# One core, attention beside a token-mixing MLP: the last K tokens ahead of the w2 load, wo in eight loads, a third oT buffer with the wo jobs spread anew

## The chip, the cores and the metric

The kernel runs on one core of a Trainium2 chip. The metric is device time in microseconds (us); lower is better. Most executions of one kernel agree within 0.3%. A difference of 2% or more counts as "faster" or "slower", less as "same". All runs named here are of the state "fast".

Engines: PE is TensorE's matrix multiplication, PEld its weight load, DVE is VectorE, ACT is ScalarE, POOL is GpSimd, SP the engine that issues nearly all transfers. "SPq" lines in the profile are instructions of SP's sequencer. PSUM is the memory, in banks, that TensorE writes its results to; a bank has to be copied out before it can be written anew. Of the names in the profile, `ps_all` is PSUM, `xs` a block of tokens before its transposition, `xnK` and `xnT` the transposed tokens, `kT` and `qT` keys and queries, `pT` the exponentials of the softmax, `ost` the weighted values as copied out of PSUM, `o_s` a unit's output and `oT` its transpose.

## The reference, cut to what matters

```python
def reference(A_x, A_wq, A_wk, A_wv, A_wo, A_beta, B_x, B_w1, B_b1, B_w2, B_b2):
    x = A_x                       # [1, 2048, 1024]
    xn = _layernorm(x, axis=-1)
    return x + _A_ref(xn, A_wq, A_wk, A_wv, A_wo, A_beta) + _B_ref(xn, B_w1, B_b1, B_w2, B_b2)
# _A_ref: 32 heads of 32, the 2048 tokens in 4 segments of 512. Per segment: causal softmax
#   attention inside the segment, plus a read of a compressive memory M, z that holds
#   elu+1 of the earlier segments' keys against their values; gated; then o @ wo.
# _B_ref: layernorm again, then a mixer over tokens: 2048 -> 3584 -> 2048 with gelu, w1, w2.
```

## The kernel before

The program has three stretches: the first mixer product (w1), the second one (w2, and with it the K projection of tokens 1024 to 2047), and attention in 32 *units* (4 segments of 8 groups of 4 heads). All engines are programmed from one place. What the whole case turns on is the order of each engine's queue: in the traces here an instruction that waits holds up what stands behind it (VectorE did nothing from 224.27 to 231.57 us before one instruction, as shown below, though the next one needed nothing that was missing after about 228.8 us, when experiment 2 runs it).

The normalised tokens for the K projection are made by `k_prepare`, which is called after each of the seven products of a w2 step. `n` counts those calls. A token block is scaled on VectorE, then transposed by a DMA. Then four differences (`kD`, operands of a fast multiplication with seven products instead of eight) are made on VectorE:

```python
    TOKENS_AT = (2, 3, 5, 6, 8, 9, 11, 12)
    def k_prepare(self, i, p):
        n = 7 * i + self.ORDER.index(p)
        if n in self.TOKENS_AT:
            ...
            self.xn_scale(c, F16)                                  # VectorE
            self.fw.dma(self.xnK[...], self.xs[c % 4][:], ..., transpose=True, own=True)
        if n - 2 in self.TOKENS_AT[:4]:
            self.xn_load(12 + self.TOKENS_AT.index(n - 2))
        n -= 7 * (self.K_FIRST - 1)
        if 0 <= n < 4:
            self.differences(self.kB, self.R_kB, self.kD, self.R_kD, (n + 1,))
        ...
```

The load of w2 for the step after next (1.8 MB) is issued at calls 5, 12, and so on, just ahead of `k_prepare`.

In attention, a unit's dense work (a queue of *jobs* of eight 512-column matmuls each: the q, k and v projections and the wo product) is cut into pieces that fill TensorE between the logits and the weighting by the softmax. Side work for VectorE is popped at certain *stops* inside the jobs:

```python
    def attention(self):
        ...
        for s in range(N_SEG - 1):
            at = [N_GRP * s + 10 + n for n in range(8)] if s < 2 else [26, 27, 28, 29, 30, 30, 31, 31]
            for n, u in enumerate(at):
                self.wo_plan.setdefault(u, []).append((4 * s + n // 2, n % 2))
        ...
        self.load_fin(0)
        self.load_fin(1)
        self.fw.dma(self.wo[:], self.A_wo.rearrange("(jc p) j -> p jc j", p=P), writes=[self.R_wo])
        for u in range(N_UNIT):
            ...
            if u in self.XN_AT[::4]:                 # u = 0, 6, 14
                self.xn_load(xn)
                self.xn_load(xn + 1)
            ...
            self.stops = self.STOPS_FEW if total <= 26 and u >= N_GRP else self.STOPS
            self.dense(cuts[0]); self.logits(u, 0); self.dense(cuts[1], end)
            if u: self.weigh(u - 1, 0)
            self.dense(cuts[2], False)
            if u: self.weigh(u - 1, 1)
            ...
```

(`STOPS_FEW` has more stops than `STOPS`, in spite of its name: it is for units with few jobs.)

## Time and profile before

| | before |
|---|---|
| median of its runs | 665.98 us |
| span of the profiled run | 664.9 us |
| PE busy | 643.0 us, 97% |
| PE idle in all | 21.9 us |

Lines of the profile page: the span, the busy time of the engines, and two rows of the 40 equal slices (16.6 us each; a digit is tenths).

```profile
span 664.9 us, 11143 instructions
...
PE 643.0 (97%) x4560; PEld 303.7 (46%) x4611; DVE 440.9 (66%) x829; ACT 281.7 (42%) x305; POOL 156.0 (23%) x181
...
PE   9999999999999999999999997999999999999987
...
PEclk9999999999999999999999997999999999999999
...
```

TensorE is the engine that bounds the kernel (97% busy), so time is to be won only where it is idle or slow. One slice, the 25th (about 399 to 416 us), shows both: PE busy falls to 7 tenths and so does the granted clock. Next, who waited for whom (engine, what and line, `<-` what ended the wait: total us, times, longest us; `issue` means that the profile names nothing that was waited for):

```profile
...
PE ps_all L198 <- DVE kT L1259: 4.1, 1, 4.1
...
PE ps_all L198 <- DVE part L690: 1.9, 1, 1.9
PE ps_all L198 <- DVE ost L1412: 1.9, 3, 1.1
...
```

The three of TensorE's waits that are shown are for VectorE. The first in time has this history. In the timeline of SP's sequencer (start, duration, what):

```profile
...
221.79 0.44 SPq L220 DMA_DIRECT2D w2s<-in_B_w_dram  x1
222.30 6.20 SPq L220 DMA_TRANSPOSE xnK<-xs  x1
...
```

and of VectorE and TensorE:

```profile
...
231.57 1.23 DVE L664 TENSOR_TENSOR kD<-xnK,xnK 128x2048 f16<-128x2048 f16 x1 [7.30 <-issue]
...
232.71 0.68 DVE L690 TENSOR_TENSOR part<-ps_all,part 128x512 f32<-128x512 f32 x1
...
233.46 2.76 PE L198 MATMUL ps_all<-g,sum 128*128 128x512 f16 x12 [1.90 <-DVE part L690]
...
```

The last K token's transpose was issued at 222.30 us, just behind a w2 load of 1.8 MB, held the sequencer for 6.2 us and landed at 231 us. VectorE had come to the first difference at 224.27 and waited 7.30 us. The view puts that wait down to "issue"; that it was for the token is read from the landing time here, and from experiment 2, where the same wait is put down to the DMA. Behind it in VectorE's queue stood an add (`part<-ps_all`) that frees what TensorE needs, so TensorE stood for 1.90 us.

The second history, at the start of attention:

```profile
...
391.00 0.43 SPq L220 DMA_DIRECT2D wo<-in_A_wo_dram  x1
391.48 1.07 SPq L220 DMA_DIRECT2D xs<-in_A_x_dram  x2
...
401.46 0.55 DVE L1131 TENSOR_SCALAR xs<-xs,ln_mv,ln_rs 128x1024 bf16<-128x1024 bf16 x1 [8.16 <-DMA xs<-in_A_x_dram]
401.93 0.68 DVE L1259 CAST kT<-ps_all 128x512 bf16<-128x512 f32 x1
...
402.76 0.58 PE L198 MATMUL ps_all<-xnT,wq 128*128 128x512 bf16 x1 [4.14 <-DVE kT L1259]
...
406.76 1.46 PE L198 MATMUL ps_all<-xnT,wq 128*128 128x512 bf16 x3
...
```

The load of wo, 2 MB, went out at 391.00 us, the two xs loads behind it at 391.48. They landed at 401.4 us, 10 us later, where the median of such loads is 3.4. VectorE waited 8.16 us to scale xs; the copy of kT stood behind that, and TensorE waited 4.14 us for the PSUM bank that this copy frees. After that, three matmuls take 1.46 us in all, where three took 0.82 elsewhere: they start some 0.43 us apart instead of 0.216. The whole stretch of units 0 and 1 (from one first exponential of an even unit to the next), in the view of stretches:

```profile
...
core 0: us, PE busy (x) PEld busy (x) DVE busy (x) ACT busy (x) POOL busy (x), PEclk, DMA share, GB/s
389.84:410.58 20.74, 15.93 (x123) 6.91 (x124) 7.39 (x18) 11.55 (x10) 4.94 (x8) 0.84 0.83 235
...
```

The mean granted clock (the third number from the end) was 0.84 there, and the pair took 20.74 us, where the next pairs take 15.0. The third of the waits, for the copy of ost, falls for the most part (1.12 us of 1.9) in units 9 and 10.

### The profile page before, as it was taken

Reading aid. Unit: us, or ns where it says so; the run is one execution under the profiler, and the core shown is the slowest. Engines: PE = TensorE matmul, PEld = TensorE weight load, DVE = VectorE, ACT = ScalarE, POOL = GpSimd, SP = SyncE. Lnnn points to the kernel's source line nnn. Section 1 sums busy time; section 2 is a strip of 40 time slices with the busy share of each in tenths; the row PEclk is TensorE's granted clock in tenths of the full one; section 3 lists DMA queues with packets and bytes.
Section 4 is the critical chain, followed back from the end, with each engine's and each line's share of the span. In section 5 each row is a group of like instructions: output and inputs, shape, how many; then the busy total and the mean of one; then the engine's idle time right before and its main releaser. Section 6 shows DMA issues by size and latency. Waiting matters only on the chain.

```text
span 664.9 us, 11143 instructions
## 1 busy us (share of the span) xinstructions
PE 643.0 (97%) x4560; PEld 303.7 (46%) x4611; DVE 440.9 (66%) x829; ACT 281.7 (42%) x305; POOL 156.0 (23%) x181
## 2 busy tenths in 40 slices
PE   9999999999999999999999997999999999999987
PEld 3444444444444444444444443444445445455443
DVE  6975766656654583563745315766988988787885
ACT  7542322322200000110110164778767778788850
POOL 2500000000021122020220211434333444444440
PEclk9999999999999999999999997999999999999999
DMA  9704242332599825727536966967654675445324
GB/s 303 205 1 127 66 125 65 92 99 64 153 251 268 214 87 151 222 65 220 146 107 175 253 178 171 157 146 155 117 128 108 152 165 143 112 112 125 94 69 129
DMA packets 190011, 95.00 MB, mean 143 GB/s; under 512 B 108552, under 2 KB 176136, under 8 KB 189960
## 3 DMA queue, kind: packets, MB, share of 16 engines
q1 hardware_dynamic: 189816, 94.25, 55.7%
q8 instruction: 36, 0.59, 0.4%
q14 instruction: 15, 0.12, 0.1%
q10 hardware_dynamic: 144, 0.03, 0.0%
HBM read 69.23 MB, written 11.53 MB: 121 GB/s over the span
## 4 chain that ended last, share of the span: by engine, by line
PE 55%; DVE 5%; issue 3%; DMA 2%; ACT 1%; SPq 0%; DVEq 0%
PE ps_all L198 55%; DMA xs<-in_A_x_dram 1%; DVE prod L1458 1%; DVE ost L1412 1%; ACT pT L1361 1%; DVE fin L1604 1%; SPq L220 0%; DMA oT<-o_s 0%; DVE fin L1304 0%; DMA xnK<-xs 0%; DVE o_s L1464 0%; DVE srec L1454 0%; DVE mtmp L1225 0%; DVE kT L1259 0%; DVE srec L1455 0%
## 5 line engine op out<-in xcount | busy, mean ns | idle before, releaser
L1361 ACT ACTIVATE pT<-ps_all 128x2048 bf16<-128x2048 f32 x80 | 150.1, 1876 | 52.4 <-PE ps_all L198 52.2
L1365 POOL TENSOR_SCALAR_AFFINE_SELECT pT<-pT 128x512 bf16<-128x512 bf16 x128 | 107.4, 856 | 168.9 <-ACT pT L1361 168.7
L690 DVE TENSOR_TENSOR part<-ps_all,part 128x512 f32<-128x512 f32 x84 | 57.7, 690 | 105.4 <-PE ps_all L198 85.0
L1076 POOL TENSOR_TENSOR part<-part,stg 128x512 f32<-128x512 f32 x24 | 33.0, 1402 | 287.1 <-DVE part L690 287.1
L747 ACT ACTIVATE g<-part,b1c 128x512 f16<-128x512 f32 x36 | 26.0, 722 | 98.8 <-DVE part L690 98.8
L198 PE MATMUL ps_all<-xnT,wq 128*128 128x512 bf16 x241 | 62.1, 386 | 5.4 <-DVE kT L1259 4.1
L198 PE MATMUL ps_all<-wo,oT 128*128 128x512 bf16 (+2 forms) x256 | 63.0, 366 | 1.8 <-DMA oT<-o_s 0.8
L198 PE MATMUL ps_all<-wv,xnT 128*128 128x512 bf16 x242 | 62.9, 380 | 0.6 <-issue 0.2
L695 ACT ACTIVATE part<-ps_all 128x512 f32<-128x512 f32 x24 | 14.0, 596 | 103.3 <-PE ps_all L198 69.2
L1412 DVE CAST ost<-ps_all 128x396 bf16<-128x396 f32 (+2 forms) x96 | 43.6, 472 | 19.6 <-PE ps_all L198 18.7
L198 PEld LDWEIGHTS ps_all<-vA,pT 128*128 128x128 bf16 x1280 | 45.8, 96 | 23.1 <-DVE ost L1412 5.8
L198 PE MATMUL ps_all<-g,sum 128*128 128x512 f16 x224 | 51.0, 379 | 1.9 <-DVE part L690 1.9
L198 PE MATMUL ps_all<-g,w2s 128*128 128x512 f16 x224 | 51.0, 379 | 0.0
L198 PE MATMUL ps_all<-vA,pT 128*128 128x33 bf16 x1280 | 48.7, 178 | 2.3 <-DVE ost L1412 1.9
L198 PE MATMUL ps_all<-gT,sum 128*128 128x512 f16 x224 | 50.3, 379 | 0.0
L198 PE MATMUL ps_all<-h,sum 128*128 128x512 f16 x192 | 45.2, 379 | 0.0
L198 PE MATMUL ps_all<-h,w1s 128*128 128x512 f16 x192 | 44.9, 379 | 0.0
L198 PE MATMUL ps_all<-hT,sum 128*128 128x512 f16 x192 | 43.6, 379 | 0.0
L198 PEld LDWEIGHTS ps_all<-xnT,wq 128*128 128x128 bf16 x256 | 23.2, 98 | 32.1 <-issue 9.4
L1458 DVE TENSOR_TENSOR prod<-ost,srec 128x1024 bf16<-128x1024 bf16 x24 | 36.8, 1533 | 0.0
L198 PE MATMUL ps_all<-qT,kT 32*128 32x384 bf16 (+3 forms) x512 | 31.9, 303 | 4.0 <-ACT pT L1361 1.9
L198 PEld LDWEIGHTS ps_all<-g,sum 128*128 128x128 f16 x224 | 21.9, 98 | 28.6 <-DVE part L690 2.6
(118 smaller groups left out, 852.6 us busy)
## 6 DMA issues: line engine op xcount, KB each, us to landing
w2s<-in_B_w_dram SPq DMA_DIRECT2D x8, 1792.0 KB, 9.1
w1s<-in_B_w_dram SPq DMA_DIRECT2D x12, 1024.0 KB, 5.6
wq<-in_A_wq_dram SPq DMA_DIRECT2D x32, 256.0 KB, 3.4
xs<-in_A_x_dram SPq DMA_DIRECT2D x24, 256.0 KB, 3.4
stg<-in_A_x_dram SPq DMA_DIRECT2D x16, 256.0 KB, 2.9
out_dram<-stg SPq DMA_DIRECT2D x16, 256.0 KB, 3.3
wk<-in_A_wk_dram SPq DMA_DIRECT2D x16, 256.0 KB, 3.7
fin<-out_dram SPq DMA_DIRECT2D x16, 256.0 KB, 3.4
```

Source lines behind the costliest of these rows:

```text
L198: ins = self.nc.tensor.matmul(*args, **kwargs)
L690: self.fw.op("dve", lambda e: e.tensor_tensor(self.tmp[dst][:], self.bank(b), self.tmp[src][:], op=ALU.add), reads=[self.R_bank[b], self.R ...
L695: self.fw.op("act", lambda e: e.activation(self.tmp[dst][:], self.bank(b), ACT.Copy), reads=[self.R_bank[b]], writes=[self.R_tmp[dst]])
L747: self.fw.op("act", lambda e: e.activation(self.gB[f % 2][half][:, f // 2, :], src, ACT.Gelu_apprx_tanh, bias=self.b1c[:, f:f + 1], scale= ...
L1076: fw.op("pool", lambda e: e.tensor_tensor(self.tmp[t][:], self.tmp[t][:], self.stg[k][:, 512 * half:512 * half + 512], op=ALU.add), reads= ...
L1361: fw.op("act", lambda e: e.activation(dst, src, ACT.Exp, scale=SCALE), reads=self.R_bank[0:4], writes=[R[v % 2][kb] for v, kb, _ in blocks ...
L1365: fw.op("pool", lambda e: e.affine_select(d, d, pattern=[[0, 4], [1, P]], compare_op=ALU.is_ge, fill=0.0, base=0, channel_multiplier=-1), ...
L1412: fw.op("dve", lambda e: e.tensor_copy(dst, src), reads=[self.R_bank[b]], writes=[self.R_ost[o][part]])
L1458: fw.op("dve", lambda e: e.tensor_tensor(self.prod[:], ost[:, :, 0:D_HEAD], rec.unsqueeze(2).to_broadcast([P, 32, D_HEAD]), op=ALU.mult), ...
L1604: fw.op("dve", lambda e: e.tensor_tensor(dst, self.ps[:, b, c0:c1], dst.bitcast(F16), op=ALU.add), reads=[self.R_bank[b], R], writes=[R])
```

## The change

The intent: take away these two stalls, and give the last four units, which have less dense work than the others, some of the wo jobs of the units before. For that the output of two segments has to be kept a little longer, hence a third buffer of `oT`. The diff, cut to its core:

```diff
-    TOKENS_AT = (2, 3, 5, 6, 8, 9, 11, 12)
+    TOKENS_AT = (2, 3, 4, 6, 8, 9, 10, 11)
@@ k_prepare
-        if 0 <= n < 4:
-            self.differences(self.kB, self.R_kB, self.kD, self.R_kD, (n + 1,))
+        if 1 <= n < 5:
+            self.differences(self.kB, self.R_kB, self.kD, self.R_kD, (n,))
@@ every use of oT
-   self.oT[s % 2] ... self.R_oT[s % 2]
+   self.oT[s % 3] ... self.R_oT[s % 3]
@@
+    WO_AT = (range(10, 18), (18, 20, 21, 22, 24, 25, 26, 28), (28, 29, 29, 30, 30, 30, 31, 31))
@@ attention
-            at = [N_GRP * s + 10 + n for n in range(8)] if s < 2 else [26, 27, 28, 29, 30, 30, 31, 31]
+            at = self.WO_AT[s]
...
-        self.load_fin(0)
-        self.load_fin(1)
-        self.fw.dma(self.wo[:], self.A_wo.rearrange("(jc p) j -> p jc j", p=P), writes=[self.R_wo])
         for u in range(N_UNIT):
+            if u == N_GRP:
+                ... take "oT2" where stg was; self.oT.append(t); self.R_oT.append(R)
+                self.load_fin(0)
+                self.load_fin(1)
+            if 1 <= u <= N_GRP:
+                self.fw.dma(self.wo[:, u - 1, :], self.A_wo[(u - 1) * P:u * P, :], writes=[self.R_wo[u - 1]])
...
-            if total <= 26:
+            if u < 10 or u >= 14 and total <= 26:
...
-            self.stops = self.STOPS_FEW if total <= 26 and u >= N_GRP else self.STOPS
+            self.stops = self.STOPS_FEW if total <= 26 and u >= 14 else self.STOPS
```

The title leaves the last two changed lines out. No unit below 14 changes its cuts (units 10 to 13 have 32 matmuls, the others at most 24), but units 8 and 9 go from the many stops to the few.

More of the change, by code (lines that the diff above doesn't have):

```diff
@@ L1181, in before_attention @@
         elif p == 2:
-            self.wo, (self.R_wo,) = take("wo", [P, N_GRP, D_MODEL], BF16)
+            self.wo, self.R_wo = take("wo", [P, N_GRP, D_MODEL], BF16, N_GRP)
         elif p == 3:
@@ L1189, in before_attention @@
             self.xnT[1], self.R_xnT[1] = take("xnT1", [P, N_DCH, SEG_L], BF16, 4)
-            w = _Walk(self.mem, self.B_AT, self.B_AT + self.STG_AT)
+            w = _Walk(self.mem, self.B_AT, self.B_AT + self.S2_AT)
             self.MZ32, self.R_MZ32 = w.take("MZ32", [P, N_GRP, GW], F32, N_GRP)
@@ L1298, in mm @@
         def mm(b, j):
-            self.fw.mm(self.bank(b), self.oT[s % 2][:, j, (c % 4) * P:(c % 4 + 1) * P],
+            self.fw.mm(self.bank(b), self.oT[s % 3][:, j, (c % 4) * P:(c % 4 + 1) * P],
                        self.wo[:, j, half * 512:(half + 1) * 512], start=(j == 0), stop=(j == N_GRP - 1))
@@ L1308, in end @@
                 self.load_fin(c + 2)
-        return [0, None, lambda: [self.R_wo] + self.R_oT[s % 2], mm, end, True]
+        return [0, None, lambda: self.R_wo + self.R_oT[s % 3], mm, end, True]
     def load_fin(self, c):
@@ L1472, in o_transpose_dma @@
         s, g, o = u // N_GRP, u % N_GRP, u % 2
-        self.fw.dma(self.oT[s % 2][:, g, :].rearrange("p (q t) -> p q t", q=4),
+        self.fw.dma(self.oT[s % 3][:, g, :].rearrange("p (q t) -> p q t", q=4),
                     self.o_s[o][:].rearrange("p q j -> p (q j)"),
-                    reads=[self.R_os[o]], writes=[self.R_oT[s % 2][g]], transpose=True)
+                    reads=[self.R_os[o]], writes=[self.R_oT[s % 3][g]], transpose=True)
     def o_transpose(self, u, b):
@@ L1483, in o_transpose @@
                 fw.tp(bb[:, q * P:(q + 1) * P], self.o_s[o][:, q, :], self.ident[:])
-        fw.op("act", lambda e: e.activation(self.oT[s % 2][:, g, :], bb, ACT.Copy),
-              reads=[self.R_bank[b]], writes=[self.R_oT[s % 2][g]])
+        fw.op("act", lambda e: e.activation(self.oT[s % 3][:, g, :], bb, ACT.Copy),
+              reads=[self.R_bank[b]], writes=[self.R_oT[s % 3][g]])
+    WO_AT = (range(10, 18), (18, 20, 21, 22, 24, 25, 26, 28), (28, 29, 29, 30, 30, 30, 31, 31))
     STOPS = ((1, 4, 7), (1, 4))
@@ L1523, in attention @@
         self.dense(100)
-        self.load_fin(0)
-        self.load_fin(1)
-        self.fw.dma(self.wo[:], self.A_wo.rearrange("(jc p) j -> p jc j", p=P), writes=[self.R_wo])
         for u in range(N_UNIT):
+            if u == N_GRP:
+                t, R = _Walk(self.mem, self.B_AT + self.STG_AT, self.B_AT + self.S2_AT).take(
+                    "oT2", [P, N_GRP, SEG_L], BF16, N_GRP)
+                self.oT.append(t)
+                self.R_oT.append(R)
+                self.load_fin(0)
+                self.load_fin(1)
+            if 1 <= u <= N_GRP:
+                self.fw.dma(self.wo[:, u - 1, :], self.A_wo[(u - 1) * P:u * P, :], writes=[self.R_wo[u - 1]])
             even = u % 2 == 0
@@ L1594, in product @@
             for p, (c0, c1) in enumerate(cols):
-                with fw.group(reads=[self.R_wo] + self.R_oT[s % 2][j0:j1], writes=[self.R_bank[b]]):
+                with fw.group(reads=self.R_wo[j0:j1] + self.R_oT[s % 3][j0:j1], writes=[self.R_bank[b]]):
                     for jc in range(j0, j1):
-                        fw.mm(self.ps[:, b, c0:c1], self.oT[s % 2][:, jc, i * P:(i + 1) * P],
+                        fw.mm(self.ps[:, b, c0:c1], self.oT[s % 3][:, jc, i * P:(i + 1) * P],
                               self.wo[:, jc, h * 512 + c0:h * 512 + c1], start=(jc == 0), stop=(jc == N_GRP - 1))
```

## The prediction

> **What bounds the kernel now.** TensorE. The page gives PE 643.0 of 664.9 us busy (97%), and the chain of waits is almost all matmuls from 233 us on. What can be won is idle or slowed TensorE time; by the stretches view, timeline and waits:
>
> 1. 231.6 to 233.5 us: PE idle 1.90 us behind a VectorE add; VectorE had waited 7.30 us to start the first difference of K's tokens (kD). The last token transpose was issued at 222.30 us, just behind the 1.8 MB w2 load, and took 9.0 us to land (median 4.9).
> 2. 398.6 to 402.8 us, units 0 and 1 of attention: PE idle 4.1 us behind a VectorE copy (kT), itself behind the scaling of xs, which waited 8.16 us for its load. It landed after 10 us (median 3.4), behind the 2 MB wo load (9.8 us). Afterwards matmuls start 0.43 us apart, not 0.216: the granted clock over 389.8 to 410.6 us is 0.84. The Trainium skill, "TensorE: Matmul & The Clock Gate" (Part 1), has the clock halved after an idle window of about 3.4 us; this trace agrees, as the 1.9 us gap did not do it. Units 0 and 1 take 20.7 us; later pairs of units of that segment take 15.0.
> 3. 472 to 474.6 us (units 9/10): PE idle about 1.5 us behind a late VectorE queue.
> 4. Units 28 to 31: pairs of 12.9 and 13.3 us with 11.4 and 11.5 us of PE work. They have 32 filler matmuls where other pairs have 48.
>
> **What the change does.**
> - K's last token is transposed ahead of the w2 load, the differences start a step later. Stall 1 goes: −1.9 us.
> - wo comes as eight 256 KB loads (like loads take 3.4 us) during units 1 to 8. Stall 2 goes with its slow clock: the pair should take 14.4 us, not 20.7: −6.3 us. The DMA share in units 2 to 9 (0.65 to 0.88) rises by about 0.16 (9.8 us over 60), transposes have a unit of slack.
> - The third oT buffer lets wo jobs wait. Pairs 18/19, 22/23 and 26/27 lose one job (8 matmuls, 1.73 us), pair 28/29 gains two, 30/31 one. Thinned pairs meet VectorE's bound (12.9 us busy of 15.5, less 0.7): about 14.0 us each, −4.2 in all. Pair 28/29 goes to about 15.1 (+2.2), 30/31 to 13.8 (+0.6). Net −1.4 us.
> - Units 8 and 9 pop side work at fewer stops, so kT's and ost's copies come earlier in VectorE's queue: perhaps −0.6 us of stall 3.
>
> All on the critical path, as PE carries the chain. Sum −10.2 us: **656.0 us**, range 652.8 to 660.0. Chances: faster by over 2% 0.11, within 2% 0.88, slower 0.01.
>
> **What the profile would show if right.** No PE gap near 231 us and no wait of kD; no gap near 399 us, granted clock 1.00 there, xs landing in about 3.5 us; units 0 and 1 in 14 to 15 us; shorter PE waits on ost near 470 us; pairs 18/19, 22/23, 26/27 shorter, 28/29 longer by 2 us. PE busy falls by about 3 us, idle by 7.
>
> **What would make it wrong.** Another stall long enough to halve the clock; wo pieces delaying the pk or xnT transposes so that TensorE waits in units 2 to 9; thinned pairs not shrinking (then the spread costs 2 us).

## The result

The changed kernel took 656.25 us (median; 656.11 to 656.45), the kernel before 665.98 (665.67 to 666.79) in the same rounds. The ratio is 0.9852, with a 95% interval of 0.9835 to 0.9869, so 1.5% less time and "same" by the 2% rule. Ratios are the mean time of one kernel's fast runs over that of the other's of the same rounds, so not quite the ratio of the medians quoted.

The same lines of the page after:

```profile
span 654.1 us, 11147 instructions
...
PE 640.9 (98%) x4560; PEld 302.8 (46%) x4611; DVE 439.7 (67%) x829; ACT 281.2 (43%) x305; POOL 156.1 (24%) x181
...
PE   8999999999999999999999999999999999999997
...
PEclk9999999999999999999999999999999999999999
...
```

PE's busy time fell by 2.1 us (it had been run slowly for a while before), its idle time from 21.9 to 13.2 us. The weak slice is gone. Of the waits:

```profile
...
PE ps_all L198 <- issue: 2.1, 13, 0.2
...
```

Of the three waits of TensorE that were shown above, those for `kT` and `part` are no longer in the list and that for `ost` is down to 0.2 us; the largest of TensorE's waits that is left is 2.1 us in 13 pieces. The K stretch after, SP first, then VectorE and TensorE:

```profile
...
217.49 4.83 SPq L220 DMA_TRANSPOSE xnK<-xs  x3
...
223.00 0.43 SPq L220 DMA_DIRECT2D w2s<-in_B_w_dram  x1
...
```

```profile
...
228.66 0.69 DVE L690 TENSOR_TENSOR part<-ps_all,part 128x512 f32<-128x512 f32 x1 [4.28 <-PE ps_all L198]
229.27 1.21 DVE L664 TENSOR_TENSOR kD<-xnK,xnK 128x2048 f16<-128x2048 f16 x1
...
231.48 0.81 PE L198 MATMUL ps_all<-g,sum 128*128 128x512 f16 x3
```

All three last transposes are ahead of the w2 load, the add comes before the difference, and TensorE goes on without a gap. The start of attention after:

```profile
...
387.91 1.06 SPq L220 DMA_DIRECT2D xs<-in_A_x_dram  x2
...
395.66 1.39 SPq L220 DMA_DIRECT2D wo<-in_A_wo_dram  x1
```

```profile
...
387.85:401.84 13.99, 13.53 (x123) 6.12 (x124) 7.48 (x18) 11.43 (x9) 4.58 (x8) 1.00 0.76 180
...
```

xs goes out first and lands in 3.2 to 3.5 us, the first of the eight wo loads follows 8 us later. The clock stays at 1.00 and the pair takes 13.99 us.

Where did it come from? The first exponential of each even unit cuts the profiled runs into pieces:

| stretch | before us | after us | difference |
|---|---|---|---|
| start to the first exponential of unit 0 | 389.84 | 387.85 | -1.99 |
| units 0, 1 | 20.74 | 13.99 | -6.75 |
| units 2 to 9 | 60.30 | 60.30 | 0.00 |
| units 10, 11 | 20.22 | 19.24 | -0.98 |
| units 12 to 17 | 50.45 | 50.45 | 0.00 |
| units 18, 19 (one wo job fewer) | 15.70 | 14.14 | -1.56 |
| units 20, 21 | 15.48 | 15.92 | +0.44 |
| units 22, 23 (one fewer) | 15.47 | 13.91 | -1.56 |
| units 24, 25 | 15.25 | 15.69 | +0.44 |
| units 26, 27 (one fewer) | 15.10 | 13.77 | -1.33 |
| units 28, 29 (two more) | 12.89 | 15.59 | +2.70 |
| units 30, 31 and the tail (one more) | 33.46 | 33.25 | -0.21 |
| all | 664.9 | 654.1 | -10.8 |

Four sources, then: K (2.0), wo (6.75), units 10 and 11 (1.0), and the spread of the wo jobs, at first sight 1.1. The first and the last row scatter from run to run: over all the profiled runs below the first exponential came at 389.84 to 390.18 us with the old K stretch and at 387.77 to 388.06 with a new one; the last row has its own story in experiment 7.

### The profile page after: what moved, and what is told of

Its sections match the earlier page's. It is cut to its first block, busy times and chain, and to the rows that moved or that the text cites. A ratio compares the mean times of both kernels' runs of the same rounds, so it can differ in the third digit from the quotient of the medians.

```text
span 654.1 us, 11147 instructions
## 1 busy us (share of the span) xinstructions
PE 640.9 (98%) x4560; PEld 302.8 (46%) x4611; DVE 439.7 (67%) x829; ACT 281.2 (43%) x305; POOL 156.1 (24%) x181
## 4 chain that ended last, share of the span: by engine, by line
PE 88%; DVE 7%; issue 2%; ACT 1%; DMA 1%; POOL 0%; DVEq 0%
PE ps_all L198 88%; DVE prod L1458 1%; DVE ost L1412 1%; ACT pT L1361 1%; DVE fin L1611 1%; DVE ln_st L588 1%; DVE fin L1304 0%; DVE o_s L1464 0%; DMA oT<-o_s 0%; DMA xin<-in_A_x_dram 0%; DVE mtmp L1225 0%; DVE h L628 0%; DVE srec L1454 0%; POOL ln_rs L612 0%; DVE mtmp L1227 0%
## 5 line engine op out<-in xcount | busy, mean ns | idle before, releaser
L198 PEld LDWEIGHTS ps_all<-wo,oT 128*128 128x128 bf16 x272 | 23.1, 97 | 26.0 <-issue 6.1
L198 PEld LDWEIGHTS ps_all<-g,sum 128*128 128x128 f16 x224 | 21.9, 98 | 26.4
```

The costliest lines, as they stand in the source:

```text
L198: ins = self.nc.tensor.matmul(*args, **kwargs)
```

## The experiments

Twelve runs were made, in three sets: the kernel before with one part of the change or with filler matmuls (warm_fill), the changed kernel with one part undone or altered, and the changed kernel itself once more. All gave correct results. Times of a set are medians beside the kernel before in the same rounds.

### 1. k_tokens: the new token steps alone

```diff
 (kernel before)
-    TOKENS_AT = (2, 3, 5, 6, 8, 9, 11, 12)
+    TOKENS_AT = (2, 3, 4, 6, 8, 9, 10, 11)
```

> The kernel before with only the new token steps; the differences stay where they were. Theory (the stall comes from the last token's transpose standing behind the 1.8 MB w2 load): the last transpose lands by about 224.5 us, the first difference waits under 1 us, the 1.90 us gap of TensorE at 231.6 us is gone, about -1.9 us in all. Rival (both halves of the K change are needed, because VectorE reaches the first difference at 224.3 us, before the token has landed): a gap of 0.5 us or more stays. Units of attention unchanged.

Measured: 663.89 us against 666.96, ratio 0.9956 (0.9938 to 0.9975). No wait of TensorE is listed between 200 and 262 us, and VectorE no longer waits before the first difference:

```profile
...
224.56 1.23 DVE L664 TENSOR_TENSOR kD<-xnK,xnK 128x2048 f16<-128x2048 f16 x1
...
231.69 1.68 PE L198 MATMUL ps_all<-g,sum 128*128 128x512 f16 x7
```

The first exponential came at 388.06 us (before: 389.84). So this half alone takes the stall away; the rival falls. The median fell by more than that, 3.1 us; in the profiled run most of the rest is in units 0 and 1, which took 19.32 us here for a reason that experiment 5 shows.

### 2. k_shift: the differences one step later, alone

```diff
 (kernel before)
-        if 0 <= n < 4:
-            self.differences(self.kB, self.R_kB, self.kD, self.R_kD, (n + 1,))
+        if 1 <= n < 5:
+            self.differences(self.kB, self.R_kB, self.kD, self.R_kD, (n,))
```

> The kernel before with only the differences one step later; the tokens' transposes stay behind the w2 load and land at about 231.3 us as before. If the stall is only a matter of what stands behind the waiting difference in VectorE's queue, then the add that TensorE needs (ready at 228.4 us) now goes first, the difference waits about 2.5 us for the token, TensorE needs nothing from VectorE before 234 us, and the whole 1.9 us is won by this half alone. Rival (the token must be early): 1 us or more of the gap stays.

Measured: 664.92 us against 666.96, ratio 0.9970 (0.9954 to 0.9987). The first exponential came at 387.98 us. VectorE and TensorE in the timeline:

```profile
...
228.79 0.69 DVE L690 TENSOR_TENSOR part<-ps_all,part 128x512 f32<-128x512 f32 x1 [4.29 <-PE ps_all L198]
...
231.61 3.19 PE L198 MATMUL ps_all<-g,sum 128*128 128x512 f16 x14
231.90 1.23 DVE L664 TENSOR_TENSOR kD<-xnK,xnK 128x2048 f16<-128x2048 f16 x1 [2.42 <-DMA xnK<-xs]
...
```

The token is as late as before (the difference waits 2.42 us for it), but TensorE has no gap, because the add it needs now stands ahead of the waiting difference. So each half of the K change wins the whole 1.9 us by itself, and together they win it once. Undoing one half of the full change would therefore have shown nothing, which is why both were tried alone.

### 3. wo_behind: still one load of 2 MB, but behind the xs loads

```diff
 (kernel before)
-        self.fw.dma(self.wo[:], ...)              # ahead of the unit loop
         for u in range(N_UNIT):
 ...
             if u in self.XN_AT[::4]:
                 self.xn_load(xn)
                 self.xn_load(xn + 1)
+                if u == 0:
+                    self.fw.dma(self.wo[:], ...)
```

> The kernel before with wo still one load of 2 MB in unit 0, but issued just behind the two xs loads instead of ahead of them. Theory (order in the queue makes the stall): the xs loads land in about 3.5 to 5 us, no gap at 399 us, granted clock 1.00, units 0 and 1 in 14 to 15.5 us instead of 20.7, about -6 us in all. Rival (the 2 MB burst itself is the trouble and must be split): the loads and transposes behind it come 6 to 10 us late and TensorE still stands for over 2 us in units 0 to 3, less than -4 us.

Measured: 660.61 us against 666.96, ratio 0.9909 (0.9890 to 0.9928). The first xs load landed after 3.9 us. Units 0 to 3 in the view of stretches:

```profile
...
389.91:403.90 13.99, 13.53 (x123) 6.12 (x124) 6.70 (x16) 11.43 (x9) 4.58 (x8) 1.00 1.05 280
403.90:419.36 15.46, 14.79 (x166) 7.35 (x168) 10.96 (x28) 11.60 (x9) 4.93 (x9) 1.00 0.99 187
...
```

Units 0 and 1 take 13.99 us, as in the changed kernel, with the clock at 1.00 and a DMA share of 1.05: the DMA engines are busy throughout, and TensorE doesn't mind. The pair after it takes 15.46 us, 0.44 more than with eight loads, and TensorE shows a wait of 0.3 us for a wq load. So in the profiled runs, of the 6.75 us that the change of the wo load wins, about 6.3 come from the order alone and 0.44 from cutting the load and moving it. (The change also moves two output loads, `load_fin`, from ahead of xs to unit 8; here they stay ahead, and units 0 and 1 take the same 13.99 us.) Not every run was that good: of the six, four have a mean granted clock of 1.000 and took 659.7 to 660.8 us, two have 0.997 and took 662.05 and 662.34. All five runs of the eight loads (experiment 4) have 1.000. So the big load may leave TensorE a risk of a slow clock that the small loads don't. What stands behind the big load is late, as the rival said (a transpose held SP for 4.77 us, where 1.2 is usual), but it has time to be late.

### 4. wo_eight: the eight loads alone

```diff
 (kernel before)
-        self.load_fin(0)
-        self.load_fin(1)
-        self.fw.dma(self.wo[:], ...)
         for u in range(N_UNIT):
+            if u == N_GRP:
+                self.load_fin(0)
+                self.load_fin(1)
+            if 1 <= u <= N_GRP:
+                self.fw.dma(self.wo[:, u - 1, :], self.A_wo[(u - 1) * P:u * P, :], writes=[self.R_wo[u - 1]])
```

> The kernel before with only the eight wo loads over units 1 to 8 (and the first two output loads in unit 8, as the change has them, since the program's check of reused DMA semaphores needs it). Theory: units 0 and 1 go from 20.74 to about 14.0 us, units 2 to 9 unchanged within 0.2 us, units 10 and 11 still 20.2 us (the stall near 474 us is a matter of the stops, not of the loads), -6.7 us in all. Rival for the last point: units 10 and 11 shrink by 1 us here already.

Measured: 660.07 us against 666.96, ratio 0.9896 (0.9876 to 0.9915). Units 0 and 1 took 13.99 us, units 2 to 9 15.02, 15.02, 15.02 and 15.25, units 10 and 11 still 20.22. All as the theory has it. (The first build of this kernel, which left the two output loads where they were, was stopped by the kernel's own assertion. It stops with "stale dma wait on slot 23: 32 vs 48": the program hands out 64 semaphores to its loads in turn, and with eight loads more, the one that VectorE would still have waited for had been reused. The move of those two loads in the change is a necessity, then, not a tuning.)

### 5. warm_fill: keep the stall, but not TensorE's idleness

```diff
 (kernel before)
             if u:
                 self.weigh(u - 1, 0)
+            if u == 1:
+                with self.fw.group(reads=[self.R_ident] + self.R_xnT[0], writes=[self.R_bank[5]]):
+                    for _ in range(18):
+                        self.fw.mm(self.bank(5), self.ident[:], self.xnT[0][:, 0, :], start=True, stop=True)
             self.dense(cuts[2], False)
```

> The kernel before, with wo still ahead of xs, and 18 extra matmuls of 512 columns (about 3.9 us at 0.216 us each) of which nothing is used, put into TensorE's queue where it stands for 4.1 us in unit 1. The wait of VectorE for xs stays. Theory (of the 6.75 us that units 0 and 1 lose, 4.1 are the stand and about 2.6 the halved clock after it): the gap is filled, the granted clock stays 1.00, units 0 and 1 take about 18.1 us instead of 20.7, -2.6 us in all, although more work is done. Rival (the slow matmuls after the gap come from a backlog on VectorE and not from the clock): units 0 and 1 stay at 20.5 us or more.

Measured: 664.17 us against 666.93, ratio 0.9961 (0.9946 to 0.9977): 18 more matmuls, and less time.

```profile
...
398.76 4.04 PE L198 MATMUL ps_all<-xnT,ident 128*128 128x512 bf16 x18
...
403.62 0.38 PE L198 MATMUL ps_all<-xnT,wq 128*128 128x512 bf16 x1 [0.81 <-DVE kT L1259]
...
```

```profile
...
390.13:408.98 18.85, 17.89 (x143) 7.79 (x142) 7.32 (x18) 11.55 (x9) 4.59 (x8) 1.00 0.91 247
...
```

The gap is filled but for 0.81 us, the clock is 1.00, and the pair takes 18.85 us. This time xs landed 0.6 us later, so the stall was 18 x 0.216 + 0.81 = 4.7 us; 13.99 + 4.7 = 18.7, and 18.85 was measured. So with a full clock the pair costs its work and the stall, and hardly anything else. In the run of before it cost 20.74 - 13.99 - 4.14 = 2.6 us on top: that is the halved clock. The same sum for k_tokens (clock 0.91, gap 4.2 us) gives 1.1 us, for k_shift (clock 0.84, gap 4.5 us) 2.7. The price of the cold clock is thus not a constant. The traces show what it depends on: the granted clock was at half for 6.8 us in the kernel before and in k_shift, but for 3.4 us in k_tokens. In the view of stretches, the kernel before and then k_tokens:

```profile
...
401.78:408.60 6.82, 5.48 (x49) 2.73 (x51) 4.63 (x13) 2.35 (x2) 0.00 (x0) 0.50 0.71 157
...
```

```profile
...
400.28:403.69 3.41, 2.69 (x35) 1.62 (x36) 1.81 (x4) 0.63 (x1) 0.00 (x0) 0.50 0.65 126
...
```

TensorE was busy for 5.48 and 2.69 us of them; half of that, 2.7 and 1.3 us, is about what was paid. That the length differs agrees with what the Trainium skill, "TensorE: Matmul & The Clock Gate" (Part 1), says of the activity window, there of a kernel's start: it runs freely, so how many matmuls are slow varies from run to run. It also explains why the profiled pair of k_tokens was shorter than that of before.

### 6. old_stops: units 8 and 9 with their old stops

```diff
 (changed kernel)
-            self.stops = self.STOPS_FEW if total <= 26 and u >= 14 else self.STOPS
+            self.stops = self.STOPS_FEW if total <= 26 and u >= N_GRP else self.STOPS
```

> The changed kernel with units 8 and 9 popping their side work at the many stops of before. Theory: the 1.1 us wait of TensorE for the ost copy near 465 us comes back, units 10 and 11 take about 20.2 us instead of 19.24, about +1.0 us in all (657.2 us), all other pairs unchanged. Rival (the wait went because of the moved loads): units 10 and 11 stay at 19.2 us.

Measured: 657.49 us (657.44 to 657.65), ratio 0.9863. The pair 10/11 takes 20.22 us again, every other pair up to 28/29 is within 0.02 us of the changed kernel (units 30, 31 and the tail are 0.3 longer, for the reason in experiment 7), and this line is back in the list of TensorE's waits from 447 to 482 us:

```profile
...
PE ps_all L198 <- DVE ost L1412: 1.1, 1, 1.1
```

So the 0.98 us come from the stops. VectorE's queue at the end of unit 9 and the start of unit 10, in the kernel before and in the changed one (the rows between are left out):

```profile
...
471.76 0.73 DVE L1464 TENSOR_TENSOR o_s<-prod 128x512 bf16<-128x512 bf16 x1
...
473.34 0.68 DVE L1259 CAST kT<-ps_all 128x512 bf16<-128x512 f32 x1
473.94 1.04 DVE L1412 CAST ost<-ps_all 128x396 bf16<-128x396 f32 x2
...
```

```profile
...
462.92 0.68 DVE L1259 CAST kT<-ps_all 128x512 bf16<-128x512 f32 x1
463.52 0.55 DVE L1412 CAST ost<-ps_all 128x396 bf16<-128x396 f32 x1
...
466.32 0.42 DVE L1464 TENSOR_TENSOR o_s<-prod 128x512 bf16<-128x512 bf16 x1
...
```

Before, the last sum of unit 8 (`o_s`) and the elementwise work on the keys stood ahead of the copies of kT and ost, which TensorE waits for. With fewer stops in unit 9 the two copies come first and `o_s` after them: the first copy of ost starts 1.4 us after the exponential of unit 10 (462.14 us), in the kernel before 3.1 us after it (470.88 us). `o_s` can be late, as its transpose is wanted by no one before unit 18.

### 7. old_spread and old_spread_again: the wo jobs where they were

```diff
 (changed kernel)
-    WO_AT = (range(10, 18), (18, 20, 21, 22, 24, 25, 26, 28), (28, 29, 29, 30, 30, 30, 31, 31))
+    WO_AT = (range(10, 18), range(18, 26), (26, 27, 28, 29, 30, 30, 31, 31))
```

> The changed kernel with the wo jobs spread as before (the third oT buffer stays). Theory: units 18 to the end take 1.1 us longer than in the changed kernel (pairs 18/19, 22/23, 26/27 longer by 1.3 to 1.6 each, 28/29 back to about 12.9), units 0 to 17 as in the changed kernel; ratio to the kernel before about 0.987 (657.3 us). Rival (the third buffer itself, by taking away waits of the transposes at units 17 and 25, brings part of it): less than 0.6 us longer.

Measured: 656.46 us (656.42 to 656.57), only 0.2 above the changed kernel's 656.25 of the earlier rounds. That was too near to tell, so the same kernel was run again beside the unaltered changed kernel:

> The changed kernel itself, unaltered, so that it stands in the same rounds as the three spreads. Expected 656.2 us, ratio 0.985.

> The changed kernel with the old spread of the wo jobs, once more, beside the changed kernel. The first run of it gave 656.46 us, only 0.2 above the changed kernel's 656.25 of another session, while by the pairs of units the spread is worth 0.87 us with one more job in the tail. Theory (the spread wins about 0.7 us): 0.5 to 1.0 us slower than the changed kernel of these rounds. Rival (what the pairs win, the last units and the tail give back): within 0.3 us of it.

Measured: 656.08 us (655.89 to 656.31) for the changed kernel, 656.36 (656.21 to 656.80) for the old spread; ratios 0.9843 and 0.9847. The profiled spans differ by 0.6 us in the first comparison and by 0.3 in the second, the medians by 0.2 (of different rounds) and 0.3. So the spread wins 0.2 to 0.6 us, and the theories of 1.1 and then 0.7 were too high; in the second comparison the rival, that the last units give most of it back, is the nearer one. The rival named before the first run, that the third buffer itself brings part of it, falls: old_spread has the third buffer, and its units 12 to 29 take the same time as those of wo_eight, which has two, within 0.02 us in each pair. From unit 18 to 29 the pairs sum to 89.89 us with the old spread and to 89.02 with the new, 0.87 less. Units 30, 31 and the tail take 33.04 and 32.86 us in the two runs with the old spread, 33.25 and 33.21 in the two with the new one, for one job more.

These last units scatter, and the traces show with what. In most runs TensorE waits there once for the transpose of an output, in the profiles of before and after:

```profile
PE ps_all L198 <- DMA oT<-o_s: 0.8, 1, 0.8
```

```profile
PE ps_all L198 <- DMA oT<-o_s: 0.5, 1, 0.5
```

With four wo jobs in the last two units (every run with the old spread) this wait is 0.9, 0.8, 0.6, 0.5, 0.4, 0.4, 0.3 and 0 us, and the last units take 33.57, 33.46, 33.16, 33.10, 33.06, 33.04, 32.86 and 32.44 us, in the same order. So the -0.21 in the table above came from a long wait in the profile of before. Why the transpose lands later in one run than in another is open.

### 8. spread2, spread2_again and spread3: can the spread be better?

```diff
 (changed kernel; spread2)
-    WO_AT = (range(10, 18), (18, 20, 21, 22, 24, 25, 26, 28), (28, 29, 29, 30, 30, 30, 31, 31))
+    WO_AT = (range(10, 18), (18, 20, 21, 22, 24, 25, 26, 28), (28, 29, 30, 30, 30, 31, 31, 31))
 (spread3)
+    WO_AT = (range(10, 18), (18, 20, 22, 24, 25, 26, 28, 28), (29, 30, 30, 30, 30, 31, 31, 31))
```

> A try at something better than the changed kernel: one wo job moved from units 28/29 to 30/31. By the changed kernel's numbers pair 28/29 loses 1.3 to 1.7 us; units 30/31 and the tail took one job at no cost (33.46 us before with four, 33.25 with five), so the sixth may cost 0.5 to 1.7 us. Expected between -1.0 and +0.3 us against the changed kernel; if TensorE is really full there by now, nothing.

> One wo job moved from units 28/29 to 30/31, once more, beside the changed kernel. By the pairs it wins 1.57 us in units 28/29 and gives back 0.9 in the last units and the tail: 0.5 to 0.9 us faster than the changed kernel of these rounds. If the first reading was chance: within 0.3 us.

> A step further: pair 20/21 thinned to one wo job as well, units 28/29 keep three, units 30/31 take seven. Pair 20/21 loses 1.1 to 1.7 us; if TensorE is full in the last units by now, the seventh job costs its whole 1.73 us there: 0.0 to +0.6 us against the kernel with six. If there is still idle time at the end, up to 0.7 us faster.

Measured: spread2 655.42 us, and again 655.47 (655.20 to 655.71) beside the changed kernel's 656.08; spread3 655.58 (655.47 to 655.63) in those same rounds. Ratios to the kernel before: 0.9832, 0.9833 and 0.9834. The changed kernel and spread2 from unit 28 on, split at the first exponential of unit 30 and at the last exponential:

```profile
...
605.26:620.85 15.59, 15.19 (x167) 7.37 (x169) 12.35 (x25) 11.40 (x9) 7.34 (x10) 1.00 0.46 119
620.85:632.44 11.59, 11.02 (x146) 5.75 (x148) 10.15 (x19) 8.02 (x6) 6.14 (x7) 1.00 0.37 102
632.44:654.10 21.66, 17.33 (x134) 9.11 (x134) 13.33 (x27) 2.47 (x2) 2.25 (x3) 0.98 0.35 111
...
```

```profile
...
605.22:619.24 14.02, 13.54 (x161) 6.65 (x160) 11.47 (x24) 11.44 (x9) 6.86 (x9) 1.00 0.50 130
619.24:632.14 12.90, 12.50 (x154) 6.20 (x153) 10.74 (x20) 8.03 (x6) 6.43 (x8) 1.00 0.32 90
632.14:653.40 21.26, 17.75 (x139) 9.57 (x137) 14.03 (x27) 2.47 (x2) 2.48 (x2) 1.00 0.36 115
...
```

Moving one job takes 1.57 us from pair 28/29 and adds 1.31 to units 30 and 31. Of their 11.59 us TensorE had been busy for 11.02, so the sixth job costs three quarters of its 1.73 us. That nets 0.26 us; the other 0.40 are in the tail, which is 21.26 us instead of 21.66 here and 21.33 instead of 21.61 in the later pair of profiles. There the wait for the output's transpose, 0.5 and 0.4 us in the changed kernel, is in the list of none of the three runs with a sixth or seventh job at the end (spread2 twice, spread3): TensorE has work while the transpose lands. spread2 beats both kernels, by about 0.6 us (0.1%) against the changed one. spread3 shows the limit: the pair 20/21 does lose 1.55 us, but 22/23 gets 0.44 longer and the last units take the rest, so nothing is won by a seventh job.

## Why the prediction was right

The prediction was 656.0 us, the measurement 656.25. Point by point:

- **What bounds the kernel**: right. TensorE's idle time and its cold clock gave all that was won; its own work is unchanged (4560 matmul instructions in both profiles). Its busy time was to fall by about 3 us and its idle time by 7; they fell by 2.1 and 8.7.
- **K, predicted -1.9**: the profiled runs show -1.99. The prediction named both halves, the earlier transpose and the later differences, and did not say that one is enough. k_tokens shows that the earlier transposes alone win it, k_shift that the later differences alone do, by letting the add that TensorE needs go first. That VectorE's work finds room in its new order was also right: no new wait in this stretch.
- **wo, predicted -6.3**: -6.75, and -6.9 by the ratio of wo_eight (0.0104 of 667 us). The prediction guessed 14.4 us for the pair; it was 13.99. The reading of the clock held: warm_fill shows the cold clock as a cost of its own, 2.6 us of the 6.75 in that run. Of the rest the order makes nearly everything (wo_behind), which the prediction did not separate. The DMA share did rise, by more than the 0.16 foreseen: 0.92, 1.03, 1.03 and 1.16 in units 2 to 9 after, 0.88, 0.65, 0.80 and 0.80 before, 0.25 higher on average. It cost TensorE nothing.
- **Spread, predicted -1.4**: the term that was mis-sized. It is worth 0.2 to 0.6 us. The thinned pairs came out as foreseen (about 14.0; measured 14.14, 13.91 and 13.77), but not for the reason given. The prediction had them meet VectorE's bound; VectorE was busy for only 10.3 to 12.0 us of each, and TensorE for 13.1 to 13.5, so TensorE still bounds them. What was missed: the full pairs behind thinned ones grew by 0.44 us each, and pair 28/29 went to 15.59, not 15.1. In the pair 20/21 TensorE's loads of weights waited 0.6 us for the ost copy, where no such wait is listed before, so a VectorE queue that comes out of the thinned pair late may be part of it; that was not tested, and the 0.44 stays unexplained.
- **Stops, predicted -0.6**: -0.98, with the mechanism shown by old_stops.
- **The sum** is near because the misses offset each other: about 0.9 too little for wo, K and the stops together, 0.8 to 1.2 too much for the spread. That it came within 0.25 us is luck; that it was near 10 us is not.

The kernel before scattered between 664.8 and 669.0 us over the later sessions, the changed kernel only between 655.9 and 656.5. The clock for each run tells most of it. Of the 31 runs of the kernel before in the three sets, the eight with a mean granted clock of 0.997 took 664.8 to 666.0 us, the 20 with 0.994 or 0.995 took 666.2 to 669.0, the two with 0.992 took 668.1 and 669.0, and one with 0.996 took 665.7. In the profiles 0.997 is one stretch of 3.4 us at half clock in units 0 and 1 (k_tokens) and 0.995 one of 6.8 us (before, k_shift). The changed kernel has 0.999 or 1.000 in every run. What decides between the short and the long stretch was not followed up.

## What to carry to other kernels

Before you cut a big load into pieces, ask what stands behind it in the queue: issuing the small load that someone waits for first gave 6.3 of 6.75 us in the profiled run here, with the big load whole (two of the six runs did less well). The same holds for an in-order compute engine: an operation that waits for a late transfer should stand behind whatever TensorE needs next, which was worth as much as making the transfer early. When idle time is moved rather than removed, as with the spread of the wo jobs, count what the receiving units give back; and try the two halves of a change alone as well as undone, since redundant halves show nothing when only one is undone.

## What the Trainium skill lacked or had wrong

- "TensorE: Matmul & The Clock Gate", Part 1, has the clock halved after an idle window of about 3.4 us that runs freely. The traces agree: gaps of 4.1 to 4.5 us brought the mean clock of the pair to 0.84 to 0.91, with half clock for 3.4 or 6.8 us, and the gap of 1.9 us did nothing. The page calls the ramp, there at a kernel's start, less than 1% of a typical span. The price of going cold in mid-kernel was less than that too (1.1 to 2.7 us of 665), but on top of each gap it is not small: from a quarter (1.1 on 4.2 us) to six tenths (2.6 on 4.1 us) of the gap itself.
- The same page advises against idle gaps of over about 3 us; it doesn't say that matmuls whose result is thrown away can fill one at a profit where the gap itself must stay: 18 of them (3.9 us of TensorE work) made the kernel 0.4% faster.
- "DMA: Bandwidth & Descriptors", section "Queues, rings and completion order", has descriptors of one ring consumed in order. The runs agree (a 256 KB load landed after 10.1 us behind the 2 MB load and after 3.9 us ahead of it). What that section gives no size for is the effect on the issuing engine: the transfer right behind a 1.8 MB load held SP's sequencer for 6.2 us (a transpose, before) or 6.4 us (a plain load of 256 KB, after), where 1.2 and 0.6 us are usual, so that everything behind it is late to be issued as well. It is no fixed rule: right behind the 2 MB load of wo, two plain loads held it for 1.07 us together (before), and it was the second transfer behind it, a transpose, that took 4.77 us in wo_behind.
